# Making the last rows of a decode kernel with VectorE transposes, and its up weights in two loads

## The chip, the cores and the metric

The kernel runs on one core of one Trainium2 chip. The metric is the device time of a whole run in microseconds (us). TensorE is called PE in the profile, VectorE DVE, ScalarE ACT, GpSimd POOL, SyncE SP; PEld is TensorE's weight load. Where a line says L460, that is line 460 of the kernel at hand; the changed kernel has the same code a few lines lower.

## The reference

One decode step of a transformer layer, batch 1, one token, in bf16:

```
h  = x + attention(layernorm(x))           # D = 1024, 32 query heads, 4 kv heads, 65536 cached keys, head size 128
h2 = h + (gelu(n @ w_gate) * (n @ w_up)) @ w_down     # n = layernorm(h);  w_gate, w_up: 1024 x 3584;  w_down: 3584 x 1024
```

The caches and weights are 173 MB, read once each. The output is one row of 1024 bf16 values, 2 KB.

## The kernel before

Every large tensor passes through one pool of five load buffers, always issued from SP:

```python
    def load(src, name):
        t = chpool.tile([P, CW], BF16, name=name, tag="ch")     # chpool: bufs=5, CW = 16384
        ...
        nc.sync.dma_start(out=tv, in_=src)
        return tv
```

The up projection accumulates over eight row blocks `c`. Its weights come in loads of four, three and one blocks (`GB` is 4), so that after the last bytes only seven matmuls are left. The result is then transposed on TensorE and multiplied with the gelu:

```python
    def up_proj(wmat, name, sizes):
        ...
        for sz in sizes:
            wv = load(wv_all[:, c0:c0 + sz, :], name + "_sb")
            for cc in range(sz):
                wide_mm(banks, hnz[:, c, :], ..., NF, c == 0, c == DC - 1)      # 7 matmuls of 512 columns
        ...
    for j0, nj, src in up_proj(B_w_up, "wu", [GB] * (DC // GB - 1) + [GB - 1, 1]):
        nc.vector.tensor_tensor(out=by_j(act_bf, j0, nj), in0=src, in1=by_j(gl, j0, nj), op=ALU.mult)
```

The down projection comes in loads of 14, 7, 4, 2 and 1 row blocks. The first 14 use 28 wide matmuls into `d_ps`, whose rows are turned into a column (`hd_cp`). The other 14 go straight into a column, `dl_ps`, 112 matmuls of one column each. The sum of the two columns is the result with value `c*128+p` on partition `p`, and has to become rows to be written:

```python
    sizes = [14, 7, 4, 2, 1]
    ...
    h2_cp = rows.tile([P, DC], F32, name="h2_cp")
    nc.vector.tensor_tensor(out=h2_cp[:], in0=dl_ps[:], in1=hd_cp[:], op=ALU.add)
    h2T_ps = ps_t.tile([DC, P], F32, name="h2T_ps", tag="T")
    nc.tensor.transpose(out=h2T_ps[:], in_=h2_cp[:], identity=ident_f[:])
    o_row = rows.tile([DC, P], BF16, name="o_row")
    nc.vector.tensor_copy(out=o_row[:], in_=h2T_ps[:])
    nc.sync.dma_start(out=out[0, 0].rearrange("(c p) -> c p", p=P), in_=o_row[:])
```

Of the kernel before, what the change touches and what calls it, by code (L numbers as in the profile page):

```python
# [9 lines left out]
ALU = mybir.AluOpType  # L10
AX = mybir.AxisListType
BF16 = mybir.dt.bfloat16
F32 = mybir.dt.float32
# [4 lines left out]
def kernel(  # L18
# [13 lines left out]
    nc = tc.nc  # L32
    P = 128
# [6 lines left out]
    DC = D // P  # L40
# [33 lines left out]
    def load(src, name):  # L74
        t = chpool.tile([P, CW], BF16, name=name, tag="ch")
        n, w = src.shape[1], src.shape[2]
        tv = t[:, 0:n * w].rearrange("p (n w) -> p n w", w=w)
        nc.sync.dma_start(out=tv, in_=src)
        return tv
# [15 lines left out]
    ident_f = const.tile([P, P], F32, name="ident_f")  # L95
# [61 lines left out]
    def wide_mm(banks, stat, mov, ns, first, last):  # L157
        for s in range(ns):
            g = s % 4
            nc.tensor.matmul(banks[s // 4][32 * g:32 * g + 32, :], lhsT=stat, rhs=mov(s),  # L160
                             start=first, stop=last, tile_position=(0, 32 * g))

    def evac(dst, src, k):
        if k % 2 == 0:
            nc.vector.tensor_copy(out=dst, in_=src)  # L165
        else:
            nc.scalar.copy(out=dst, in_=src)  # L167
# [20 lines left out]
    for hf in range(2):  # L188
        for t in range(2):
            o = W2 * hf + rep * t  # L190
            nc.vector.tensor_copy(out=qsel[64 * t:64 * t + 64, :, :, hf, o:o + rep],
                                  in_=qsel_ps[64 * t:64 * t + 64, :, :].rearrange("p a (g h) -> p g a h", h=rep))
# [154 lines left out]
    rows = ctx.enter_context(tc.tile_pool(name="rows", bufs=1))  # L347
    ps_w = ctx.enter_context(tc.tile_pool(name="ps_w", bufs=4, space=PSUM))
    ps_t = ctx.enter_context(tc.tile_pool(name="ps_t", bufs=3, space=PSUM))
    DS = D // 512  # L350

    def row_bank(name):
        return ps_w.tile([P, 512], F32, name=name, tag="w")
# [12 lines left out]
    for wc in range(Hq // WN):  # L366
        wv = load(wo_v[:, wc * WN:(wc + 1) * WN, :], "wo_sb")
        for cc in range(WN):
            c = wc * WN + cc
# [14 lines left out]
    def cp_sum(row, add, name):  # L384
        ps = ps_t.tile([P, 4, DS], F32, name=name + "_ps", tag="T")
        for b in range(4):
            nc.tensor.matmul(ps[:, b, :], lhsT=row[:, b * P:(b + 1) * P], rhs=hsel[:], start=True, stop=True)
        t = rows.tile([P, DC], F32, name=name)
        nc.vector.tensor_tensor(out=t[:].rearrange("p (s b) -> p b s", b=4), in0=ps[:],
                                in1=add[:].rearrange("p (s b) -> p b s", b=4), op=ALU.add)  # L390
        return t
# [4 lines left out]
    GB = CW // F  # L396
    NF = FC // 4

    def up_proj(wmat, name, sizes):
        banks = [row_bank(name + "_ps") for _ in range(2)]  # L400
        wv_all = wmat.rearrange("(p c) n -> p c n", c=DC)
        c0 = 0
# [3 lines that stand above are left out]
                c = c0 + cc  # L406
                wide_mm(banks, hnz[:, c, :],
                        lambda s, w=wv[:, cc, :]: w.rearrange("p (m j) -> p m j", j=FC)[:, :, 4 * s:4 * s + 4],
                        NF, c == 0, c == DC - 1)
            c0 += sz  # L410
        assert c0 == DC
        outs = []
        for k in range(2):
            ng = min(4, NF - 4 * k)
            ev = rows.tile([P, 512], F32, name=name + "_ev", tag=f"ev{k}")
            evac(ev[0:32 * ng, :], banks[k][0:32 * ng, :], k)
            t_ps = ps_t.tile([P, 4, P], F32, name=name + "_t", tag="T")
            for b in range(4):
                nc.tensor.transpose(out=t_ps[:, b, 0:32 * ng], in_=ev[0:32 * ng, b::4],
                                    identity=ident_f[0:32 * ng, 0:32 * ng])  # L420
            outs.append((16 * k, 4 * ng, t_ps[:, :, 0:32 * ng:32]))
        return outs

    def by_j(t, j0, nj):
        return t[:, j0:j0 + nj].rearrange("p (g b) -> p b g", b=4)
# [11 lines left out]
    gl = rows.tile([P, FC], F32, name="gl")  # L437
    nc.vector.tensor_tensor(out=gl[:], in0=th[:], in1=g_ap[:], op=ALU.mult)
    act_bf = rows.tile([P, FC], BF16, name="act_bf")
    for j0, nj, src in up_proj(B_w_up, "wu", [GB] * (DC // GB - 1) + [GB - 1, 1]):  # L440
        nc.vector.tensor_tensor(out=by_j(act_bf, j0, nj), in0=src, in1=by_j(gl, j0, nj), op=ALU.mult)

    wd_v = B_w_down.rearrange("(p c) n -> p c n", p=P)
# [4 lines left out]
    d_ps = row_bank("d_ps")  # L448
    dl_ps = ps_w.tile([P, DC], F32, name="dl_ps", tag="w")
    nc.vector.memset(dl_ps[:], 0.0)  # L450
    c0 = 0
    for sz in sizes:
        wv = load(wd_v[:, c0:c0 + sz, :], "wd_sb")
        for cc in range(sz):
            c = c0 + cc
# [7 lines left out]
        if c0 == NW:  # L463
            d_r = rows.tile([P, 512], F32, name="d_r")
            nc.vector.tensor_copy(out=d_r[:], in_=d_ps[:])
            hd_cp = cp_sum(d_r, h_cp, "hd_cp")
    h2_cp = rows.tile([P, DC], F32, name="h2_cp")
    nc.vector.tensor_tensor(out=h2_cp[:], in0=dl_ps[:], in1=hd_cp[:], op=ALU.add)
    h2T_ps = ps_t.tile([DC, P], F32, name="h2T_ps", tag="T")
    nc.tensor.transpose(out=h2T_ps[:], in_=h2_cp[:], identity=ident_f[:])  # L470
    o_row = rows.tile([DC, P], BF16, name="o_row")
    nc.vector.tensor_copy(out=o_row[:], in_=h2T_ps[:])
    nc.sync.dma_start(out=out[0, 0].rearrange("(c p) -> c p", p=P), in_=o_row[:])


# [28 lines left out]
```

## Time and profile before

| | |
|---|---|
| time, median of 3 runs | 412.27 us (412.26 to 412.43) |
| span in the profile | 410.5 us |
| end of the last sum to issue of the output DMA | 0.82 us (407.52 to 408.34) |
| issue of the output DMA to end of span (410.478 in the trace) | 2.14 us |

The page of the kernel before, three lines: the span, the busy share of the DMA engines in tenths for 40 equal slices, and what was read.

```profile
span 410.5 us, 6349 instructions
...
DMA  8999999999999999999999999999999999999994
...
HBM read 173.02 MB, written 0.00 MB: 422 GB/s over the span
```

The stream of bytes runs at 8 to 9 tenths until the last slice: time is decided by the stream, and then by what is left to do when the last bytes are there.

The chain of waits of the kernel before, that is the work that ended last followed backwards, here printed forwards from the down weights on. Columns: start in us, duration in us, what.

```profile
372.76 25.63 DMA wd_sb<-in_B_w_down_dram
...
398.43 3.20 PE d_ps L358 x28
...
402.40 1.86 PE hd_cp_ps L387 x8
404.27 3.06 PE dl_ps L460 x112
```

The chain waits for the first down load until 398.39; from then on PE and DVE take turns. The next view, the timeline of the same kernel, shows the end in single groups. Columns: start, duration, engine, line, operation, output and input, count, and in brackets how long the engine had been idle and for whom.

```profile
387.84 3.60 PE L160 MATMUL wu_ps<-wu_sb,hnz 128*32 128x512 bf16 x28 [3.02 <-DMA wu_sb<-in_B_w_up_dram]
...
393.21 0.20 DVE L154 COPY actz<-act_bf 128x14 bf16<-128x14 bf16 x1
...
407.35 0.17 DVE L468 TENSOR_TENSOR h_cp<-dl_ps,hd_cp 128x8 f32<-128x8 f32 x1 [2.87 <-PE dl_ps L460]
...
407.57 0.38 PE L470 MATMUL h2T_ps<-ident_f,h_cp 128*8 128x128 f32 x1 [0.26 <-DVE h_cp L468]
407.99 0.28 DVE L472 CAST o_row<-h2T_ps 8x128 bf16<-8x128 f32 x1 [0.47 <-PE h2T_ps L470]
408.34 0.35 SPq L473 DMA_DIRECT2D out_dram<-o_row  x1
```

All 28 up matmuls of the last two loads run in one piece from 387.84, since the load of one block landed while the load of three was being used. The last up matmul ends at 391.44, and `actz`, the input of the down matmuls, is ready at 393.41, five us before its weights come. At the end, the sum ends at 407.52; a TensorE transpose and a cast follow; SP issues the output at 408.34. These two spots are what the change touches.

Busy time by stretches of the kernel before. After the colon pair come the length in us and, for each engine, busy us with the number of instructions; the last three columns are granted TensorE clock (1.00 is full), DMA share and GB/s.

```profile
core 0: us, PE busy (x) PEld busy (x) DVE busy (x) ACT busy (x) POOL busy (x), PEclk, DMA share, GB/s
...
393.00:396.00 3.00, 0.41 (x4) 0.33 (x3) 0.57 (x3) 0.00 (x0) 0.00 (x0) 1.00 0.93 401
396.00:398.40 2.40, 0.00 (x0) 0.00 (x0) 0.00 (x0) 0.00 (x0) 0.00 (x0) 0.59 0.95 407
...
402.00:403.00 1.00, 0.60 (x3) 0.60 (x4) 0.35 (x1) 0.00 (x0) 0.00 (x0) 0.50 0.97 399
...
404.00:405.00 1.00, 1.00 (x35) 1.00 (x35) 0.17 (x1) 0.00 (x0) 0.00 (x0) 0.50 0.54 219
...
406.00:407.00 1.00, 1.00 (x41) 1.00 (x39) 0.00 (x0) 0.00 (x0) 0.00 (x0) 0.50 0.15 51
```

Two things are to be seen here. TensorE's clock is full from 393 on and back at half when the down weights come. And the stream does not end at once: the mean share of the 16 DMA engines falls from 0.97 to 0.15 over the last 4 to 5 us, although all loads had been issued by 391.8. The last down piece (issued at 391.48, 15.4 us to landing in the DMA list) lands at 406.9.

### The profile page before, as it was taken

To read this page: it belongs to the slowest core of one execution; us is meant where nothing else is said; L and a number is where in the kernel's file an instruction comes from. 1 tells how busy PE (TensorE), PEld (TensorE's weight loads), DVE (VectorE), ACT (ScalarE), POOL (GpSimd) and SP (SyncE) were. 2 spreads that over 40 slices of the span, in tenths; PEclk is the share of its full clock that TensorE was granted. 3 is DMA by queue.
4 is the path that set the end of the run, shared out by engine and by line. 5 is a ranking of instruction groups with operands and counts; after the bars stand their busy time and mean duration, and the time that the engine had idled before them with its cause. 6 is when DMAs were issued, how large, how long until landed. Compare 5 with 4: busy or idle time off the path is not lost.

```text
span 410.5 us, 6349 instructions
## 1 busy us (share of the span) xinstructions
PE 297.7 (73%) x2705; PEld 195.3 (48%) x2705; DVE 167.6 (41%) x292; ACT 168.0 (41%) x281; POOL 5.1 (1%) x16
## 2 busy tenths in 40 slices
PE   0438989889688987496988929888987466466546
PEld 0216656655365654464565617465654223163225
DVE  0213565557256545265556535456545101021011
ACT  0013766653855654733655634455754700000000
POOL 1100000000000000000000000000000001000000
PEclk9986999999999999599999966999999585568565
DMA  8999999999999999999999999999999999999994
GB/s 358 409 460 407 460 408 457 407 454 414 439 428 429 434 417 449 416 449 410 449 420 441 423 441 426 431 433 426 437 426 437 422 445 422 434 430 433 429 418 174
DMA packets 6828, 173.43 MB, mean 422 GB/s; under 512 B 912, under 2 KB 912, under 8 KB 1296
## 3 DMA queue, kind: packets, MB, share of 16 engines
q1 hardware_dynamic: 6640, 173.02, 98.1%
q8 instruction: 21, 0.34, 0.3%
q14 instruction: 7, 0.06, 0.0%
q10 hardware_dynamic: 160, 0.00, 0.0%
HBM read 173.02 MB, written 0.00 MB: 422 GB/s over the span
## 4 chain that ended last, share of the span: by engine, by line
PE 51%; DMA 20%; DVE 14%; issue 8%; ACT 6%; POOL 0%; SPq 0%; POOLq 0%; ACTq 0%; DVEq 0%
PE kt_ps L220 26%; PE qk_ps L245 11%; DMA k_sb<-in_A_k_cache_dram 7%; DMA wd_sb<-in_B_w_down_dram 6%; DMA v_sb<-in_A_v_cache_dram 6%; DVE sc_sb L256 5%; PE acc_ps L300 5%; ACT pT L283 4%; PE sct_ps L253 4%; DVE mx L257 4%; DVE kt_sb L227 3%; ACT qk_sb L250 2%; PE o_ps L316 1%; PE wg_ps L160 1%; PE d_ps L358 1%
## 5 line engine op out<-in xcount | busy, mean ns | idle before, releaser
L220 PE MATMUL kt_ps<-ident_f,k_sb 128*128 128x128 f32 x1024 | 148.1, 288 | 17.4 <-DVE kt_sb L227 13.0
L225 ACT COPY kt_sb<-kt_ps 128x1024 bf16<-128x1024 bf16 x116 | 116.4, 1013 | 91.7 <-PE kt_ps L220 63.0
L220 PEld LDWEIGHTS kt_ps<-ident_f,k_sb 128*128 128x128 f32 x1024 | 117.5, 147 | 55.5 <-issue 21.3
L227 DVE COPY kt_sb<-kt_ps 128x1024 bf16<-128x1024 bf16 x140 | 94.6, 687 | 76.1 <-PE qk_ps L245 42.6
L245 PE MATMUL qk_ps<-kt_sb,qsel 128*32 128x512 bf16 x512 | 65.1, 395 | 7.7 <-DVE kt_sb L227 7.7
L256 DVE COPY sc_sb<-sct_ps 128x512 f32<-128x512 f32 x32 | 34.2, 1068 | 46.1 <-PE sct_ps L253 43.7
L283 ACT ACTIVATE pT<-sc_sb,nbias 128x256 bf16<-128x256 f32 x64 | 31.5, 493 | 20.6 <-DVE nbias L275 20.6
L300 PE MATMUL acc_ps<-v_sb,pT 128*32 128x512 bf16 x512 | 33.7, 407 | 3.7 <-DMA v_sb<-in_A_v_cache_dram 3.7
L250 ACT COPY qk_sb<-qk_ps 128x512 f32<-128x512 f32 x32 | 18.8, 589 | 24.9 <-PE qk_ps L245 16.5
L245 PEld LDWEIGHTS <-qsel 128*32 128x32 bf16 x512 | 15.1, 94 | 26.2 <-issue 23.8
L253 PE MATMUL sct_ps<-ident_f,qk_sb 128*128 128x128 f32 x128 | 19.9, 278 | 8.6 <-ACT qk_sb L250 8.6
L300 PEld LDWEIGHTS <-pT 128*32 128x32 bf16 x512 | 14.7, 102 | 18.5 <-issue 7.1
L257 DVE TENSOR_REDUCE mx<-sc_sb 128x8 f32<-128x512 f32 x32 | 22.0, 686 | 1.0
L253 PEld LDWEIGHTS sct_ps<-ident_f,qk_sb 128*128 128x128 f32 x128 | 14.3, 140 | 13.6 <-ACT qk_sb L250 13.6
L167 ACT COPY wg_ev<-wg_ps 96x512 f32<-96x512 f32 x1 | 0.6, 581 | 45.9 <-PE wg_ps L160 45.9
L309 PE MATMUL l_ps<-lpart,ones_f 128*128 128x8 f32 x16 | 3.7, 306 | 15.8 <-ACT pT L283 15.8
L358 PE MATMUL at_ps<-wo_sb,o2z 128*32 128x512 bf16 x64 | 7.1, 619 | 8.1 <-DMA wo_sb<-in_A_wo_dram 8.1
L160 PE MATMUL wu_ps<-wu_sb,hnz 128*32 128x512 bf16 x56 | 7.2, 625 | 7.8 <-DMA wu_sb<-in_B_w_up_dram 7.8
L160 PEld LDWEIGHTS <-hnz 128*32 128x32 bf16 x112 | 4.8, 123 | 16.0 <-issue 13.7
L283 ACT ACTIVATION_READ_ACCUMULATOR pT<-sc_sb,nbias 128x1 f32 x64 | 11.9, 187 | 0.0
L167 ACT ACT_TABLE_LOAD x1 | 1.3, 1283 | 25.0 <-DVE q_ev L165 25.0
L309 PEld LDWEIGHTS l_ps<-lpart,ones_f 128*128 128x128 f32 x16 | 3.0, 234 | 17.8 <-ACT pT L283 17.4
(126 smaller groups left out, 98.4 us busy)
## 6 DMA issues: line engine op xcount, KB each, us to landing
k_sb<-in_A_k_cache_dram SPq DMA_DIRECT2D x16, 4096.0 KB, 30.4
v_sb<-in_A_v_cache_dram SPq DMA_DIRECT2D x16, 4096.0 KB, 19.3
wq_sb<-in_A_wq_dram SPq DMA_DIRECT2D x2, 4096.0 KB, 16.7
wo_sb<-in_A_wo_dram SPq DMA_DIRECT2D x2, 4096.0 KB, 29.6
wg_sb<-in_B_w_gate_dram SPq DMA_DIRECT2D x2, 3584.0 KB, 36.4
wu_sb<-in_B_w_up_dram SPq DMA_DIRECT2D x1, 3584.0 KB
wd_sb<-in_B_w_down_dram SPq DMA_DIRECT2D x1, 3584.0 KB, 25.6
wu_sb<-in_B_w_up_dram SPq DMA_DIRECT2D x1, 2688.0 KB, 38.1
```

The costliest lines, as they stand in the source:

```text
L160: nc.tensor.matmul(banks[s // 4][32 * g:32 * g + 32, :], lhsT=stat, rhs=mov(s), start=first, stop=last, tile_position=(0, 32 * g))
L220: nc.tensor.transpose(out=kt_ps[:, b, :], in_=k32s[m0 // 16][:, m0 % 16, :], identity=ident_f[:])
L225: nc.scalar.copy(out=dst_bf, in_=src_bf)
L227: nc.vector.tensor_copy(out=dst_bf, in_=src_bf)
L245: nc.tensor.matmul(qk_ps[32 * c:32 * c + 32, :], lhsT=qsel[:, g, par, hf, :], rhs=mv[:, :, :, par], start=(hf == 0 and par == 0), stop=(hf ...
L250: nc.scalar.copy(out=qk_sb[:], in_=qk_ps[:])
L253: nc.tensor.transpose(out=sct_ps[:, b, :], in_=qk_sb[:, b * P:(b + 1) * P], identity=ident_f[:])
L256: nc.vector.tensor_copy(out=sl.rearrange("p h (m t) -> p m t h", t=2), in_=src_v)
L257: nc.vector.tensor_reduce(out=st["mx"][:, :, pi], in_=sl, axis=AX.X, op=ALU.max)
L283: nc.scalar.activation(out=pT[:, :, r, :], in_=sc_sb[:, r, hf * HG * TG:(hf + 1) * HG * TG].rearrange("p (a t) -> p a t", t=TG), func=ACT. ...
L300: nc.tensor.matmul(acc[32 * c:32 * c + rep * TG, :], lhsT=pTs[a // HG][:, a % HG, :, :].rearrange("p r t -> p (r t)"), rhs=v_sb[:, i * TG: ...
L358: nc.tensor.matmul(bank[32 * g:32 * g + 32, :], lhsT=stat, rhs=w2[:, s * 512:(s + 1) * 512], start=first, stop=last, tile_position=(0, 32 ...
```

## The change

The intent: take the round trip through TensorE and PSUM out of the tail by letting VectorE, which has made the sum, turn it too; and make one DMA fewer of the up weights.

```diff
-    for j0, nj, src in up_proj(B_w_up, "wu", [GB] * (DC // GB - 1) + [GB - 1, 1]):
+    for j0, nj, src in up_proj(B_w_up, "wu", [GB] * (DC // GB)):
...
+    o_blk = rows.tile([P, 32], BF16, name="o_blk")
+    nc.vector.memset(o_blk[:], 0.0)
+    o_tr = rows.tile([32, P], BF16, name="o_tr")
...
-    h2_cp = rows.tile([P, DC], F32, name="h2_cp")
-    nc.vector.tensor_tensor(out=h2_cp[:], in0=dl_ps[:], in1=hd_cp[:], op=ALU.add)
-    h2T_ps = ps_t.tile([DC, P], F32, name="h2T_ps", tag="T")
-    nc.tensor.transpose(out=h2T_ps[:], in_=h2_cp[:], identity=ident_f[:])
-    o_row = rows.tile([DC, P], BF16, name="o_row")
-    nc.vector.tensor_copy(out=o_row[:], in_=h2T_ps[:])
-    nc.sync.dma_start(out=out[0, 0].rearrange("(c p) -> c p", p=P), in_=o_row[:])
+    nc.vector.tensor_tensor(out=o_blk[:, 0:DC], in0=dl_ps[:], in1=hd_cp[:], op=ALU.add)
+    for i in range(4):
+        nc.vector.transpose(out=o_tr[:, 32 * i:32 * i + 32], in_=o_blk[32 * i:32 * i + 32, :])
+    nc.sync.dma_start(out=out[0, 0].rearrange("(c p) -> c p", p=P), in_=o_tr[0:DC, :])
```

## The prediction

> **What bounds the kernel now.** The page: 173 MB read at 422 GB/s over a span of 410.5 us, the DMA row at 8 to 9 tenths in every slice but the last. By stage (stretches table), the DMA share is 0.95 to 1.06 from 340 to 401.7 us, so the up and down weights land when the byte stream reaches them, not when somebody asks. The chain of waits ends: `wd_sb` DMA until 398.39, `d_ps` matmuls 3.20 us, `d_r` 0.70, `hd_cp_ps` 1.86, `dl_ps` 3.06 (to 407.33), sum 0.18, TensorE transpose 0.39, cast 0.28, output DMA issued at 408.34. The change touches the 0.82 us from the end of the sum (407.52) to that issue, and work that ends before 398.4.
>
> **Up weights in two loads.** Bytes are the same, so I expect the first down load still to land near 398.4. What moves is the PE work behind the last up bytes. Now it is 28 matmuls in one run, 387.84 to 391.44, since the load of one row block arrives while the three-block load is being used. 896 KB at about 430 GB/s after 387.8 gives an estimate of 389.9 for the joined load; its 28 matmuls at the cold 3.6 us end near 393.5, and `actz`, 1.97 us after the last up matmul in the timeline, is ready near 395.5 instead of 393.4. The down weights come at 398.4: about 2.9 us of slack, cost zero. The five load buffers shift by one: the first down load is issued near 359.2 instead of 372.76, the last near 393.5 instead of 391.5. There are megabytes queued at both times; no gain, no bubble.
>
> A side effect: TensorE stays busy closer to 398.4. Granted clock (fine stretches) is 1.00 from 393.0 to 396.3, then 0.50 again before `d_ps`. The Trainium skill, "TensorE: Matmul & The Clock Gate", section "What's actually happening", has the gate drop after an idle window of about 3.4 us; the trace agrees (393.0 to 396.4). Two us later activity may keep `d_ps` at full clock, saving up to 1.7 us there. But the last down pieces land at 406.9 (issue 391.5 plus 15.4), and `dl_ps` already ends at 407.33, so at most 0.2 to 0.3 us survives. I count 0.1.
>
> **The tail.** Removed: PE transpose and cast with hand-offs, 407.52 to 408.27. Added: four 32x32 VectorE transposes. If they overlapped like the four `esel` copies of one quadrant (starts 0.10 us apart in the opening timeline) they would cost 0.5 us. But they read partitions 0, 32, 64, 96. "VectorE: DVE Perf Modes", section "Two Vector instructions with no wait between them", says an instruction whose start quadrant differs from the last read is held until earlier ones finish. The trace agrees: the four `qsel` casts, alternating partitions 0 and 64, run strictly in turn, 0.93 us. Small VectorE operations take 0.16 to 0.23 us; with 0.02 between, four transposes take 0.75 to 0.95 us. I expect the issue 0.95 us after the sum instead of 0.82: +0.1 us. The early memset of `o_blk` (0.07 us) sits in a VectorE wait.
>
> **Prediction.** 412.3 us, range 411.5 to 413.0. Faster by over 2%: 0.5%; within 2%: 99%; slower: 0.5%.
>
> **Right if** the first down load still lands at 398.2 to 398.7; PE waits for it after `actz` is ready; the transposes are four pieces without overlap, 0.75 to 0.95 us in all; everything before 340 us is unchanged.
>
> **Wrong if** an earlier queued down load reorders the stream and delays the up weights; the transposes overlap or cost 0.3 us each; the warm clock removes more of the tail than the last landing allows; or the load sizes change the skew between DMA engines, which ends the stream at 402 to 407 us.

The two groups that the prediction compares, from two timeline views of VectorE of the kernel before, look like this. First two `esel` copies, which read and write the same partitions:

```profile
15.59 0.28 DVE L113 COPY esel<-ident_bf 128x64 bf16<-128x64 bf16 x2
```

Then the four `qsel` casts, which alternate between partitions 0 and 64:

```profile
28.17 0.93 DVE L191 CAST qsel<-qsel_ps 64x64 bf16<-64x64 f32 x4 [0.31 <-PE qsel_ps L185]
```

Two copies of 0.18 us each fit into 0.28 us; four casts of 0.22 us each need 0.93 us.

## The result

| | before | change |
|---|---|---|
| median of 6 runs of the same rounds | 412.35 us (412.17 to 413.30) | 412.87 us (412.42 to 413.77) |
| ratio, 95% interval | | 1.0011 (0.9995 to 1.0028) |
| span of the profiled run | 410.5 us | 410.6 us |
| sum's end to output issue | 0.82 us | 0.95 us |

Ratios here are the mean time of one kernel's fast runs over that of the other's fast runs of the same rounds, so not quite the ratio of the medians. The median of the change is 0.57 us over the predicted 412.3 because three of its six runs lie at 413.3 to 413.8 and three at 412.4; what that is worth comes below.

The chain of waits of the change, the lines that answer to those of before:

```profile
359.75 38.66 DMA wd_sb<-in_B_w_down_dram
...
398.46 3.20 PE d_ps L358 x21
...
402.43 1.86 PE hd_cp_ps L387 x8
404.30 3.11 PE dl_ps L463 x112
```

The first down load is now issued at 359.75 instead of 372.76, and lands at the same time: `d_ps` starts at 398.46 instead of 398.43. The chain behind it has the same pieces. The timeline of the change:

```profile
390.00 3.16 PE L160 MATMUL wu_ps<-wu_sb,hnz 128*32 128x512 bf16 x28 [4.92 <-DMA wu_sb<-in_B_w_up_dram]
...
394.76 0.20 DVE L154 COPY actz<-act_bf 128x14 bf16<-128x14 bf16 x1
...
407.43 0.17 DVE L470 TENSOR_TENSOR o_blk<-dl_ps,hd_cp 128x8 bf16<-128x8 f32 x1 [2.93 <-PE dl_ps L463]
407.63 0.84 DVE L472 STREAM_TRANSPOSE o_tr<-o_blk 32x32 bf16<-32x32 bf16 x4
408.55 0.36 SPq L473 DMA_DIRECT2D out_dram<-o_tr  x1
```

The joined up load is used from 390.00 on, its last matmul ends at 393.16, and `actz` is ready at 394.96, 1.55 us later than before but still 3.5 us ahead of its weights. In the tail four transposes take 0.84 us, one of 0.20 us every 0.21 us, and the output is issued at 408.55, 0.95 us after the end of the sum (407.60).

Stretches of the change, columns as before:

```profile
core 0: us, PE busy (x) PEld busy (x) DVE busy (x) ACT busy (x) POOL busy (x), PEclk, DMA share, GB/s
...
393.00:396.00 3.00, 1.36 (x11) 1.13 (x9) 1.28 (x4) 0.58 (x1) 0.00 (x0) 1.00 0.97 416
396.00:398.40 2.40, 0.00 (x0) 0.00 (x0) 0.00 (x0) 0.00 (x0) 0.00 (x0) 0.50 0.92 392
...
406.00:407.00 1.00, 1.00 (x41) 0.98 (x37) 0.00 (x0) 0.00 (x0) 0.00 (x0) 0.50 0.22 70
```

Two half-us stretches of the same trace show when the clock rose and fell:

```profile
392.50:393.00 0.50, 0.50 (x9) 0.14 (x3) 0.01 (x1) 0.00 (x0) 0.00 (x0) 0.93 1.19 516
...
395.50:396.00 0.50, 0.00 (x0) 0.00 (x0) 0.00 (x0) 0.00 (x0) 0.00 (x0) 0.98 0.93 401
```

The clock is back at half before the down weights come, as before, and the stream dies away in the same way. Of the 0.21 us by which the output issue is later in the two profiles, 0.13 are the longer tail and 0.08 a later sum. The span differs by 0.1 only, since from the issue to the end of the span it took 2.03 us here (span 410.578 in the trace) and 2.14 in the profile before. All eight profiles of the experiments that have two up loads and one output DMA show 2.03 to 2.05 us; the two profiles with three up loads, before and e1 below, show 2.14 and 2.20. So this 0.1 us may be an effect of the change, of its loads; no experiment was made for it.

### The profile page after: what moved, and what is told of

The parts are those of the page before. It is cut to its first block, busy times and chain, and to the rows that moved or that the text cites. A ratio compares the mean times of both kernels' runs of the same rounds, so it can differ in the third digit from the quotient of the medians.

```text
span 410.6 us, 6350 instructions
## 1 busy us (share of the span) xinstructions
PE 297.3 (72%) x2704; PEld 194.9 (47%) x2704; DVE 168.3 (41%) x296; ACT 168.1 (41%) x281; POOL 5.1 (1%) x16
## 4 chain that ended last, share of the span: by engine, by line
PE 51%; DMA 24%; DVE 14%; ACT 7%; issue 2%; SPq 0%; DVEq 0%; ACTq 0%
PE kt_ps L220 26%; PE qk_ps L245 11%; DMA wd_sb<-in_B_w_down_dram 9%; DMA k_sb<-in_A_k_cache_dram 7%; DMA wo_sb<-in_A_wo_dram 7%; DVE sc_sb L256 6%; PE acc_ps L300 5%; ACT pT L283 5%; PE sct_ps L253 4%; DVE mx L257 4%; DVE kt_sb L227 3%; ACT qk_sb L250 2%; PE at_ps L358 1%; PE o_ps L316 1%; PE d_ps L358 1%
```

## The experiments

All ten give the right result. A run at 412.9 us or more is called late here; for the kernel before the late runs reach 414.95. This line is drawn between the two clusters. The table holds every timed run, with before over all rounds and the change over both of its jobs.

| kernel | early runs, us | late runs |
|---|---|---|
| before | 412.17 to 412.84 (25) | 14 of 39 |
| the change | 412.19 to 412.84 (8) | 3 of 11 |
| e1_tail_only | 412.47 to 412.70 (3) | 3 of 6 |
| e2_loads_only | 412.14 to 412.54 (5) | 1 of 6 |
| e3_four_dmas | 412.57 to 412.88 (5) | 0 of 5 |
| e5_extra_other | 413.09 to 413.19 (3) | 414.66 besides |
| e6_extra_same | 412.63 to 412.78 (4) | 0 of 4 |
| e7_warm | 412.17 to 412.40 (5) | 1 of 6 |
| e8_bf16_pe and e10_bf16_again | 411.87 to 412.58 (10) | 1 of 11 |
| e9_bf16_warm | 411.98 to 412.49 (5) | 1 of 6 |

(In e5 the added work moves the early cluster itself over the line.)

### e1_tail_only: the transposes, with the old three loads

```diff
-    ... up_proj(B_w_up, "wu", [GB] * (DC // GB)):
+    ... up_proj(B_w_up, "wu", [GB] * (DC // GB - 1) + [GB - 1, 1]):
```

> The four VectorE transposes alone; the up weights stay in three loads. My theory: the whole lasting cost of the change is in the tail, so the profile shows the output DMA issued 0.95 us after the end of the last sum (before: 0.82), and the first down load lands as before, near 398.4 us. The time would be 0.1 us over before, which the times of whole runs cannot resolve. Runs near 413.3 us should then come about as often as in before (1 in 6), not 3 in 6. Rival: the transposes cost more than the gap between sum and issue shows, for example by a longer output write; then issue to end of span grows beyond the 2.1 us of before.

Measured: median 412.81 us, ratio 0.9992 (0.9972 to 1.0013). The profile was taken in a late run (span 412.0), which is of more use than an early one. Its timeline:

```profile
399.68 3.18 PE L358 MATMUL d_ps<-wd_sb,actz 128*32 128x512 bf16 x28 [5.28 <-DMA wd_sb<-in_B_w_down_dram]
...
408.83 0.84 DVE L472 STREAM_TRANSPOSE o_tr<-o_blk 32x32 bf16<-32x32 bf16 x4
409.75 0.37 SPq L473 DMA_DIRECT2D out_dram<-o_tr  x1
```

The tail is the same as with the change: 0.84 us of transposes, issue 0.95 us after the sum's end (408.80). What is late is the stream: `d_ps` waits for its weights until 399.68, 1.25 us longer than before. In that trace the second load of `wo` was used at 356.15, within 0.1 us of the repeat of the change, and the first up load at 382.73 instead of 381.45: the stream lost its 1.2 us between those two points. So the late run is made before the tail begins. The part of the expectation on late runs failed (3 of 6 against the "1 in 6" of before), but before itself then showed 5 late runs of 11 in the same job. From the issue to the end of the span it took 2.20 us, longer than before's 2.14, as the rival says. But the five other profiles with the transposes and one output DMA, all with two up loads, show 2.03 to 2.05, so the transposes are not the cause. In before, e1 and the change alike the packets of the write start 0.8 us after the issue: what is longer here comes later, and its cause is open.

### e2_loads_only: two loads, with the old tail

```diff
-    ... up_proj(B_w_up, "wu", [GB] * (DC // GB - 1) + [GB - 1, 1]):
+    ... up_proj(B_w_up, "wu", [GB] * (DC // GB)):
```

> The two up loads alone; the old TensorE transpose and cast. My theory: no cost. The last up matmul ends near 393.0 us instead of 391.4, the first down load still lands near 398.4, d_ps starts there, and the gap from sum to issue is 0.82 us. Median 412.2 to 412.5. Rival: the changed loads bring the runs near 413.3 us that the change shows in 3 of 6; then this kernel shows them as often and its mean is 0.4 us or more over before, and a trace of such a run shows a later landing of the first or last down load.

Measured: median 412.35 us, ratio 0.9987 (0.9967 to 1.0008); one late run of six. The timeline:

```profile
395.27 0.20 DVE L154 COPY actz<-act_bf 128x14 bf16<-128x14 bf16 x1
...
398.38 3.18 PE L358 MATMUL d_ps<-wd_sb,actz 128*32 128x512 bf16 x28 [2.74 <-DMA wd_sb<-in_B_w_down_dram]
...
408.38 0.36 SPq L473 DMA_DIRECT2D out_dram<-o_row  x1
```

The inputs are ready at 395.47, TensorE then still waits 2.74 us for the weights, `d_ps` starts at 398.38, and the tail is 0.82 us again (sum's end 407.56). The two loads cost nothing: the 2 us of extra work behind the last up bytes lie in a wait. The rival is not supported.

### e3_four_dmas: one transpose for all four blocks

```diff
+    o_tr = rows.tile([P, 32], BF16, name="o_tr")
...
-    for i in range(4):
-        nc.vector.transpose(out=o_tr[:, 32 * i:32 * i + 32], in_=o_blk[32 * i:32 * i + 32, :])
-    nc.sync.dma_start(out=out[0, 0].rearrange("(c p) -> c p", p=P), in_=o_tr[0:DC, :])
+    nc.vector.transpose(out=o_tr[:], in_=o_blk[:])
+    for q in range(4):
+        eng = nc.sync if q % 2 == 0 else nc.scalar
+        eng.dma_start(out=out[0, 0].rearrange("(c p) -> c p", p=P)[:, 32 * q:32 * q + 32], in_=o_tr[32 * q:32 * q + DC, :])
```

> One VectorE transpose of the whole 128x32 block, which turns the four 32x32 blocks each in its own partitions, in place of four; the result then lies in four groups of 8 partitions and is written by four DMAs of 0.5 KB, two issued from SP and two from ScalarE. If the cost of the tail is the four VectorE instructions in turn, one takes 0.2 us and the first issue comes 0.3 us after the sum, the second on each queue 0.35 to 0.5 us later, and the span ends 0.2 to 0.3 us earlier than with the change, if a 0.5 KB write in 64 byte pieces takes no longer than the 2 KB one in 256 byte pieces. Rival: small pieces or the extra completions take longer and the span ends later, by 0.3 us or more.

Measured: median 412.62 us (412.57 to 412.88), ratio 0.9990 (0.9970 to 1.0010). The timeline:

```profile
407.87 0.21 DVE L471 STREAM_TRANSPOSE o_tr<-o_blk 128x32 bf16<-128x32 bf16 x1
408.12 0.65 ACTq L474 DMA_DIRECT2D out_dram<-o_tr  x2
408.16 0.72 SPq L474 DMA_DIRECT2D out_dram<-o_tr  x2
```

One instruction on 128 partitions turns all four blocks in 0.21 us, as long as one block alone. The first output is issued 0.28 us after the sum's end (407.84), as expected, but the last only begins near 408.6, and the span ends 3.2 us after the sum, against 3.0 with the change. In the same job the median of the change (e4, below) was 412.28 us, 0.34 us lower; in the two profiles 0.21 us of the difference lie before the tail (e3's sum starts at 407.67, e4's at 407.46). The expected gain of 0.2 to 0.3 us is a loss of 0.2 after the sum: the four writes cost more than the three transposes saved. The rival was right about the direction, though not its 0.3 us. No run has a single DMA that picks the four groups of partitions, so that stays open.

By chance this profile has TensorE at full clock from 402 to 405 us, and it then shows two waits of `dl_ps` for down pieces (0.31 and 0.27 us). This led to e7.

### e4_after_again: the change, unaltered

> The change unaltered, to see how often its runs fall near 413.3 us. If the two clusters (412.4 and 413.3 to 413.8) are scatter that both kernels share, before and this show them about equally often in these rounds, and the ratio is 1.0003 (0.13 us of the tail). If the change makes the late cluster more likely, this shows it in about half of its runs and before in few.

Measured: median 412.28 us (412.19 to 412.84), no late run of five, ratio 0.9984 (0.9964 to 1.0005), where before had 5 late runs of 11. Over both jobs the change has 3 late of 11 and before 14 of 39. That is no sign that the change makes late runs likelier, though eleven runs cannot exclude a moderate effect. In the profile the tail is 0.95 us again.

### e5_extra_other and e6_extra_same: what the transposes wait for

Both put four more transposes, into a scratch tile, between the sum and the real four. They differ in which partitions those read:

```diff
+    o_x = rows.tile([32, P], BF16, name="o_x")
+    for i in range(4):
+        nc.vector.transpose(out=o_x[:, 32 * i:32 * i + 32], in_=o_blk[32 * i:32 * i + 32, :])   # e5
+        nc.vector.transpose(out=o_x[:, 32 * i:32 * i + 32], in_=o_blk[0:32, :])                 # e6, in its place
```

> The change, with four more VectorE transposes ahead of the four, into a scratch tile, reading partitions 0, 32, 64, 96 in turn like the real ones. With the change the four take 0.84 us in turn, 0.21 us from start to start. Both theories: eight in turn, 1.68 us, output issue 1.8 us after the end of the sum, run 0.84 us later than the change, about 413.2 to 413.3 us where the change runs at 412.4.

> The same, but the four extra transposes all read partitions 0 to 31. My theory, held because the start quadrant differs from the last read: the four extra ones and the first real one overlap, with starts about 0.1 us apart as the esel copies have them, and the three last are held; the eight take 1.15 to 1.3 us. Rival, a VectorE transpose always waits for the one before it: eight in turn, 1.68 us as in the run with other partitions.

The timeline of e5:

```profile
407.50 0.84 DVE L473 STREAM_TRANSPOSE o_x<-o_blk 32x32 bf16<-32x32 bf16 x4
408.36 0.84 DVE L475 STREAM_TRANSPOSE o_tr<-o_blk 32x32 bf16<-32x32 bf16 x4
409.27 0.36 SPq L476 DMA_DIRECT2D out_dram<-o_tr  x1
```

The timeline of e6:

```profile
407.67 0.48 DVE L473 STREAM_TRANSPOSE o_x<-o_blk 32x32 bf16<-32x32 bf16 x4
408.09 0.80 DVE L475 STREAM_TRANSPOSE o_tr<-o_blk 32x32 bf16<-32x32 bf16 x4
408.96 0.36 SPq L476 DMA_DIRECT2D out_dram<-o_tr  x1
```

With the partitions in turn, eight transposes take 1.70 us, all one after another. With the same partitions, four take 0.48 us (starts some 0.09 us apart), and the first real one, at 408.09, still overlaps them; the other three, which change partitions, come at 0.21 us again. Together 1.22 us, inside the 1.15 to 1.3 expected. The instruction, its shape, its type and the start partition of its output are the same, so the rival, that VectorE's transposes never overlap, has fallen: it is the change of the start partition of the input that makes them wait.

Whole runs follow: e5's median is 413.14 us (ratio to before 1.0019, 1.0001 to 1.0036), e6's 412.67 (0.9999, 0.9986 to 1.0012). Their difference, 0.47 us, is the one between the gaps from sum to issue, 1.79 and 1.32 us. The tail lies on the critical path in full, and what is added there is paid.

### e7_warm: TensorE kept at full clock

```diff
+    warm_ps = ps_m.tile([P, 448], F32, name="warm_ps", tag="misc")
+    for i in range(17):
+        nc.tensor.matmul(warm_ps[:], lhsT=ident_bf[:], rhs=actz[:].rearrange("p n w -> p (n w)"), start=True, stop=True)
     d_ps = row_bank("d_ps")
```

> The change, with 17 scratch TensorE matmuls of 128x448 after the up weights' transposes, so that TensorE is busy from about 395 us until the first down load lands near 398.4. It should then be at full clock for d_ps: 1.6 us instead of 3.2, and hd_cp_ps 1.0 instead of 1.86. My theory: the last down pieces land at 406.9 to 407.2 us whatever TensorE does, so dl_ps shows idle time that ends with a wd_sb landing, ends at 407.1 to 407.4, and the kernel gains at most 0.3 us. Rival: the end is TensorE's own chain from the first down landing on; then the sum comes 2.4 us earlier and the time falls to about 410 us. If the scratch matmuls run cold they overrun[...] and d_ps starts up to 3 us late; then the end is later by up to that.

Measured: median 412.23 us (early runs 412.17 to 412.40, one late), ratio 0.9998 (0.9980 to 1.0015). The timeline:

```profile
398.44 1.69 PE L358 MATMUL d_ps<-wd_sb,actz 128*32 128x512 bf16 x28
...
402.60 1.60 PE L466 MATMUL dl_ps<-act_bf,wd_sb 128*128 128x1 bf16 x56 [0.61 <-DMA wd_sb<-in_B_w_down_dram]
...
405.02 1.01 PE L466 MATMUL dl_ps<-act_bf,wd_sb 128*128 128x1 bf16 x32 [0.82 <-DMA wd_sb<-in_B_w_down_dram]
...
406.24 0.99 PE L466 MATMUL dl_ps<-act_bf,wd_sb 128*128 128x1 bf16 x24 [0.21 <-DMA wd_sb<-in_B_w_down_dram]
407.27 0.17 DVE L473 TENSOR_TENSOR o_blk<-dl_ps,hd_cp 128x8 bf16<-128x8 f32 x1 [5.07 <-PE dl_ps L466]
```

The clock stayed at 1.00 from 396 to 403, and `d_ps` took 1.69 us instead of 3.18, `hd_cp_ps` 1.05 instead of 1.86. Of these 2.3 us all but 0.16 is lost again, 1.64 of it in waits: `dl_ps` now waits 0.61, 0.82 and 0.21 us for down pieces, and the sum starts at 407.27, against 407.43 in the change. Even this 0.16 us is not clear of scatter: in the eight early-run profiles with TensorE at half clock to the end the sum starts between 407.23 and 407.47. So the end has two bounds that lie within 0.2 us or so: TensorE's own chain from the first down landing, and the landing of the last piece. A faster TensorE gives no more than that here. The rival, 2.4 us, has fallen.

### e8_bf16_pe, e10_bf16_again and e9_bf16_warm: a shorter tail

The sum is written as bf16, so that TensorE transposes bf16 and the copy out of PSUM is bf16 to bf16; up weights in two loads. e10 is e8 once more; e9 adds the scratch matmuls of e7.

```diff
-    h2_cp = rows.tile([P, DC], F32, name="h2_cp")
+    h2_cp = rows.tile([P, DC], BF16, name="h2_cp")
...
-    h2T_ps = ps_t.tile([DC, P], F32, name="h2T_ps", tag="T")
-    nc.tensor.transpose(out=h2T_ps[:], in_=h2_cp[:], identity=ident_f[:])
+    h2T_ps = ps_t.tile([DC, P], BF16, name="h2T_ps", tag="T")
+    nc.tensor.transpose(out=h2T_ps[:], in_=h2_cp[:], identity=ident_bf[:])
```

> The two up loads with the old TensorE tail, but the sum written as bf16, transposed as bf16 into a bf16 PSUM tile and copied out. The output is bf16 anyway, so the result is the same. A candidate for a shorter tail than either kernel: the float32 transpose took 0.38 us and the cast 0.28; the bf16 transpose of the attention output took 0.29 and its copy 0.21. I expect the issue 0.65 to 0.75 us after the sum (before 0.82, change 0.95), and a time within scatter of before, about 0.1 us under the two-loads run.

> The bf16 TensorE tail with two up loads once more, in the same rounds. If its gain is real its early runs fall again at 412.0 us, 0.3 us under the early cluster of before. Whether a run falls into the late cluster is not under the kernel's control by my theory, so one or two of six may be near 413.

> The candidate that joins what helped: two up loads, the bf16 TensorE transpose, and the scratch matmuls that keep TensorE at full clock. The last landing still sets the sum, 0.1 to 0.3 us earlier than without the scratch matmuls. Transpose and copy at full clock or not: issue 0.6 to 0.65 us after the sum. Most runs at 411.8 to 412.0 us, so 0.4 us under before's cluster at 412.3; not separable from the bf16 tail alone by whole runs.

The timeline of e8:

```profile
407.61 0.27 PE L470 MATMUL h2T_ps<-ident_bf,h_cp 128*8 128x128 bf16 x1 [0.26 <-DVE h_cp L468]
407.92 0.21 DVE L472 COPY o_row<-h2T_ps 8x128 bf16<-8x128 bf16 x1 [0.36 <-PE h2T_ps L470]
408.20 0.36 SPq L473 DMA_DIRECT2D out_dram<-o_row  x1
```

Transpose 0.27 us instead of 0.38, copy 0.21 instead of 0.28, issue 0.64 us after the sum's end (407.56), just under the 0.65 to 0.75 expected, where before needs 0.82 and the change 0.95. e8: median 412.03 us (411.96 to 412.03), ratio 0.9982 (0.9970 to 0.9994). e10: median 412.25 us (411.87 to 413.63), ratio 0.9990 (0.9972 to 1.0007), tail again 0.64 us; three of its five early runs lie at 412.08 or less, as expected, two at 412.41 and 412.58. The first ratio lies clear of 1, but partly because before had late runs in its rounds and e8 none. The 0.2 us of the tail are shown by the profiles; that whole runs gain more than this is not. e9 gave 412.05 us (411.98 to 413.08), ratio 0.9985 (0.9967 to 1.0002): no better than e8, so its expectation of a sum 0.1 to 0.3 us earlier failed. In its profile, which is of the slowest early run (412.49), the up matmuls ended later and the scratch matmuls ran until 399.3, when `d_ps` began; even so `dl_ps` waited for landings, and the sum started at 407.76. The four runs at 411.98 to 412.05 left no profile.

## Why the prediction was right, point by point

- **What bounds the kernel**: right. `d_ps` starts at 398.43 before and 398.46 with the change, although the first down load is issued 13 us earlier. The condition "everything before 340 us is unchanged" holds for the code, but not to the tenth in the profiles: the last load of the value cache is used at 336.78 with the change and at 336.54 before, in code that is the same. By 398 us this is gone.
- **Up weights in two loads cost zero**: right, by e2. The estimate of 393.5 for the end of the up matmuls was 0.3 us too late, since the clock rose during them (3.16 us instead of 3.6), and 395.5 for `actz` was 0.5 us too late. In e2 the clock stayed at half, and there they were 393.5 and 395.47.
- **The clock**: wrong. The step "Two us later activity may keep `d_ps` at full clock" did not happen; `d_ps` took 3.18 us. I had read the Trainium skill ("TensorE: Matmul & The Clock Gate", "What's actually happening") as asking for a whole idle window of 3.4 us before the clock falls. In the change's trace it fell near 396.0, 1.1 us after TensorE's last matmul (394.94) and about 3.4 us after it had risen (half-us stretches: 0.93 in 392.5 to 393.0, 0.98 in 395.5 to 396.0, 0.50 after). The trace of before: there too only the full clock lasted 3.4 us (393.0 to 396.4), while TensorE had been without a matmul for 3.0 (since 393.40). The 0.1 us counted for this gain did not come. Without it the prediction is 412.4, where the early runs of its own job lie (412.42 to 412.44), but 0.1 us is less than whole runs can tell.
- **The cap on that gain, 0.2 to 0.3 us**: right, by e7, where a full clock moved the sum by 0.16 us at most.
- **The tail, 0.95 us instead of 0.82**: right to the hundredth in the profiles of the change (three of them, e1 included). The reason is right too, by e5 against e6: the Trainium skill ("VectorE: DVE Perf Modes", "Two Vector instructions with no wait between them") says that an instruction is held when its start quadrant, a group of 32 partitions, differs from the last one read; the runs agree, with 0.21 us from start to start across quadrants and about 0.09 within one.
- **The memset**: right. It took 0.07 us at 343.29, in a wait of VectorE for TensorE.
- **Not in the prediction**: the late runs. They raised the first median by 0.4 us (412.43 without them), nearly out of the range of 411.5 to 413.0; one more late run of the six would have put the median outside it. That the first result fell inside was luck in part. One late run was caught: it is a stream 1.2 us late between 356 and 382 us, in a kernel with the old loads. The change and before do not differ clearly here (3 of 11 and 14 of 39). Over all kernels, though, three up loads have 17 late runs of 45 and two have 7 of 49 (without e5). The line between early and late was drawn afterwards and no experiment was made for it, so whether two loads make late runs rarer is open. Why the stream falls behind in some runs is not settled; only one late trace exists.

## What to carry to other kernels

Count instructions by what they wait for, not by what they do: four VectorE transposes on four quadrants cost 0.84 us in turn, while one transpose on all 128 partitions takes 0.21 us (but leaves its result in four groups of partitions, which e3 then had to write one by one); a TensorE round trip in bf16 gave the output 0.3 us sooner than the four. Work that ends before a transfer lands is free to move as long as it stays ahead of it, and a faster engine ahead of the last landing only waits longer. When an effect is 0.1 us and the runs fall into clusters 1 us apart, read it in the profile and use whole runs only to see that nothing larger is hidden.

## What the Trainium skill lacked or had wrong

- "VectorE: DVE Perf Modes", "The three transpose paths" and "Rules for kernel authors": times are given for 128x128 alone, and VectorE is called the fastest for 32x32. One block took 0.20 us here; no run sets a TensorE transpose of one block beside it. For four blocks in different quadrants VectorE needs 0.95 us from sum to output issue, and the TensorE round trip 0.64 (bf16) to 0.82 us (float32). A 128x32 block in one instruction took 0.21 us.
- The same page, "Two Vector instructions with no wait between them": the rule of start quadrants holds for transposes as well, with 0.21 against about 0.09 us from start to start; the page gives no times.
- "TensorE: Matmul & The Clock Gate", "What's actually happening": it has the clock fall after an idle window of about 3.4 us. Here it fell 1.1 us after the last matmul, about 3.4 us after it had risen, with TensorE busy for 1.86 us of the 3.5 before (392.5 to 396.0).
- "DMA: Bandwidth & Descriptors": no figure there for how a long stream ends. Here the mean share of the 16 engines fell from 0.97 at 402 us to 0.15 at 406 to 407 us. Nor does any page tell of whole runs that fall about 1 us behind (14 of 39 runs of the kernel before).
